# One maximum and one exponential for each head of a cached decode, with keys and values loaded apart

## The chip, the core and the metric

The kernel runs on one core of one Trainium2 chip. TensorE (PE) multiplies matrices, VectorE (DVE) reduces and combines, ScalarE (ACT) takes exponentials, GpSimd (POOL) does almost nothing here; the SyncE queue (SP) and the ScalarE queue issue the DMA transfers. A product of two float32 matrices appears in the trace as two matmul records, each with a weight load (PEld) of its own. The metric is the device time in microseconds (us) from one execution; lower is better.

## The reference

One token passes four residual layers: attention, MLP, attention, MLP, with the same weights both times. Of the attention, 32 heads of 128 numbers look at 8192 cached keys and values each:

```python
x = x + _A_ref(_layernorm(x), A_k_cache, A_v_cache, A_wq, A_wo)
x = x + _B_ref(_layernorm(x), B_w1, B_w2)
# and both once more
q = (x @ wq).reshape(B, Sq, H, Dh).transpose(0, 2, 1, 3)
scores = einsum("bhqd,bhkd->bhqk", q, k_cache) * (Dh ** -0.5)
o = einsum("bhqk,bhkd->bhqd", softmax(scores), v_cache)
attention = o.reshape(B, Sq, H * Dh) @ wo
mlp = maximum(x @ w1, 0) @ w2
```

The width of x is 640, the MLP's hidden width 1728. One head's keys and values are 8 MiB in float32, all heads together 256 MiB, and both attention layers read all of them.

## The kernel before

**The ring.** All keys and values go through one large SBUF buffer (`ring`, L70), which has room for 3712 "columns"; a column is 8 numbers in each of 128 partitions (4 KiB in all). `UNITS` (L33) cuts each head's 2048 columns (COLS, a quarter of the keys, since four groups of 32 PE columns each take a quarter) into units; a unit is one DMA and holds keys and values of the same columns side by side. A usual head has two units of two "steps" of 512 columns; the first and the last heads have smaller ones, down to 128. `place` (L81) looks for the smallest gap that holds the next unit, and `pump` (L90) issues loads on the SP queue as long as there is one; `release` (L112) frees a step's place when its values have been used, and pumps again. All this runs when the program is written, so the order of releases and loads is fixed; on the chip, a load waits until the last reader of its place has finished. Layer 0 takes heads 0 to 31, layer 1 takes them from 31 down, and what layer 0 loaded last (`KEPT`, L39, exactly one ring full: all of head 31 and most of head 30) isn't loaded again. Nothing can be loaded between the last byte of layer 0 and the first release in layer 1.

**A step** (L265) runs through these helpers: `scores` (L293) multiplies the query with the keys. For a step of 512 columns these are 16 products of 128 columns into one PSUM tile: four groups of 32 partitions, and in each of them four "rows", that is four runs of 128 keys; the query sits in column r of a 32-wide weight tile otherwise zero (`spread_q`, L287), so run r lands in row r. `maxima` (L314) takes the maximum over 128 numbers and joins it with the one of the steps before; `exponentials` (L321) takes exp with the sum, and the factor by which earlier steps have to be rescaled. `turn` (L341) transposes the 128 probabilities by a product with a 0/1 matrix and copies them to SBUF (`pT`). `values` (L357) multiplies with the values: four products of 512 columns, whose result holds for each row all four runs, of which only the row's own block counts. `rescaled` (L375) multiplies the output and the sum so far with the factor, and `gathered` (L391) adds the row's own blocks, one DVE instruction for each of four.

**A head's end.** `combined` (L418) finds the common maximum of all rows by a product that spreads them and a minimum, weighs the rows by exp, sums them by two more products and divides. That is a "chore": generators in two lists, `chores` and `slow`, which advance by one step between other work (`work_off`, L521). Other chores are the queries of the next four heads (L530), the output projection of four heads (L536), what the MLP needs before the last head is ready (`before_last`, L544) and a product of MLP weights with the last head's output weights (L444, L471), so that behind the last head there is only one product left for the MLP's hidden layer (L638).

**The order of the work** is written by hand (`manual_schedule`) and each engine takes its instructions in that order. The loop at L601 is pipelined over steps: the turn of step i, then scores, maximum and exponential of step i+1, then the values of step i, then chores and the rescaling. Behind the last step come the output of the last head (`o`, in the trace `c_ol`, L634), the rest of the MLP (L637 to L704), and in layer 0 the normalisation and first queries of layer 1 (L506 to L508), whose result is `qT` (L251).

Of the kernel before, what the change touches and what calls it, by code (L numbers as in the profile page):

```python
# [30 lines left out]

COLS = SK // 4
UNITS = {h: [[512, 512], [512, 512]] for h in range(H)}  # L33
UNITS[0] = [[128], [128], [256], [512], [512, 512]]
UNITS[29] = [[512, 512], [512], [512]]
UNITS[30] = [[256], [128], [128], [512], [512, 512]]
UNITS[31] = [[512, 512], [512], [256], [128], [128]]
RING = 3712
KEPT = [(30, i) for i in range(2, 5)] + [(31, i) for i in range(5)]  # L39
STEPS = 8  # L40
# [3 lines left out]
def rows(n):  # L44
    return 4 if n % 512 == 0 else 1
# [10 lines left out]
def decode_kernel(ctx: ExitStack, tc: tile.TileContext, x, kv, wq, wo, w1, w2, out):  # L56
# [5 lines left out]
    ps_s = ctx.enter_context(tc.tile_pool(name="ps_s", bufs=3, space=bass.MemoryType.PSUM))  # L62
# [9 lines left out]
    assert KEPT == order[len(order) - len(KEPT) :]  # L72
    todo = [(0, u) for u in order] + [(1, u) for u in order[::-1][len(KEPT) :]]
    dram_at, o = {}, 0
    for h, i in order:
        dram_at[h, i] = o
        o += 8 * P * sum(UNITS[h][i])
# [12 lines left out]
    def pump():  # L90
        while todo:
            layer, u = todo[0]
            steps = UNITS[u[0]][u[1]]
            n = sum(steps)
# [9 lines left out]
            for t, m in enumerate(steps):  # L104
                live[layer, u, t] = at, m
                at_of[layer, u, t] = 8 * at
                at += m

    def key(st):
        return (0 if st.u in KEPT else st.L), st.u, st.t  # L110

    def release(st):  # L112
        if st.L or st.u not in KEPT:
            del live[key(st)]
            pump()

# [40 lines left out]
    wct = consts.tile([P, NB, P], F32, name="wct")  # L157

# [106 lines left out]
    class Step:  # L265
        def __init__(self, L, u, t, e):
            self.L, self.u, self.t, self.e = L, u, t, e
            self.h = u[0]
            self.n = UNITS[self.h][u[1]][t]
            self.rows = rows(self.n)  # L270
            self.m = self.n // self.rows
            self.counts = ind[:, 4:5] if self.rows == 4 else ind[:, :1]

    class Head:

        def __init__(self):
            self.nm = work.tile([P, STEPS], F32, name="h_nm", bufs=2)
            self.l = work.tile([P, STEPS], F32, name="h_l", bufs=2)  # L280
            self.c = work.tile([P, STEPS], F32, name="h_c", bufs=2)
            self.sum = work.tile([P, 1], F32, name="h_sum", bufs=2)
            self.o = work.tile([P, DH], F32, name="h_o", bufs=2)

    heads_of = {}
# [7 lines left out]
    def scores(st):  # L293

        h = st.h
        st.at = at_of[key(st)]
        st.ps = bank_tile()
        for r in range(st.rows):
            for g in range(4):
                if st.rows == 1:  # L300
                    q = qT[h // HG][:, h % HG : h % HG + 1].to_broadcast([P, 32])
                else:
                    q = spread_q[h % 2][:, 3 - r : 35 - r]
                k = st.at + g * st.n + r * st.m
                nc.tensor.matmul(  # L305
                    st.ps[32 * g : 32 * g + 32, : st.m],
                    q,
                    ring[:, k : k + st.m],
                    start=(r == 0),
                    stop=(r == st.rows - 1),  # L310
                    skip_group_check=True,
                )

    def maxima(st):  # L314
        e, nm = st.e, heads_of[st.h].nm
        to = work.tile([P, 1], F32, name="s_nm", bufs=2) if e else nm[:, :1]
        nc.vector.tensor_reduce(to, st.ps[:, : st.m], AX.X, ALU.max, negate=True)  # L317
        if e:
            nc.vector.tensor_tensor(nm[:, e : e + 1], nm[:, e - 1 : e], to, op=ALU.min)  # L319
# [178 lines left out]
    def attention_and_mlp(L, xr, s):  # L498
# [92 lines left out]
        def begin(i):  # L591
            st = steps[i]
            if st.e == 0:
                due(st.h)
# [190 lines left out]
```

## Time and profile before

| what | value |
|---|---|
| median of 3 runs | 1428.64 us (1428.23 to 1429.79) |
| the profiled execution | 1427.12 us, of which 1425.3 us from the first to the last instruction (the span) |
| busy share of the span | PE 66%, PEld 39%, DVE 46%, ACT 13% |
| mean granted TensorE clock | 0.808 of full speed |
| DMA | 572.69 MB, mean 402 GB/s over the span |

In a row of the timeline the first number is the start in us from the span's start, the second its length, then engine, line, operation, result and operands, and how many records were merged (x). In a group's row stand, behind the bar, busy us and mean ns of one record, then the idle time of the engine just before them and what ended it. Records of matmuls overlap, since four groups of PE columns work side by side: x8 of the 512-column shape are four products, and the time of all eight is what counts.

### The profile page before, as it was taken

To read this page: it belongs to the slowest core of one execution; us is meant where nothing else is said; L and a number is where in the kernel's file an instruction comes from. 1 tells how busy PE (TensorE), PEld (TensorE's weight loads), DVE (VectorE), ACT (ScalarE), POOL (GpSimd) and SP (SyncE) were. 2 spreads that over 40 slices of the span, in tenths; PEclk is the share of its full clock that TensorE was granted. 3 is DMA by queue.
4 is the path that set the end of the run, shared out by engine and by line. 5 is a ranking of instruction groups with operands and counts; after the bars stand their busy time and mean duration, and the time that the engine had idled before them with its cause. 6 is when DMAs were issued, how large, how long until landed. Compare 5 with 4: busy or idle time off the path is not lost.

```text
span 1425.3 us, 30398 instructions
## 1 busy us (share of the span) xinstructions
PE 936.8 (66%) x12964; PEld 559.3 (39%) x12964; DVE 654.2 (46%) x2793; ACT 186.7 (13%) x821; POOL 2.9 (0%) x10
## 2 busy tenths in 40 slices
PE   5665546667566767666688666666657667666678
PEld 3333324344343434334345333434434344344434
DVE  2443424545444444446436544545444545445453
ACT  1111101111111111111112111111111111111110
POOL 0000000000000000000000000000000000000000
PEclk8777867888877878889768887878888887888887
DMA  9999999999999999999718999999999999999990
GB/s 398 432 432 426 428 434 428 422 427 425 425 428 428 430 419 430 431 424 423 323 53 357 427 431 430 425 429 427 419 432 431 426 421 424 431 429 427 417 418 6
DMA packets 25343, 572.69 MB, mean 402 GB/s; under 512 B 2804, under 2 KB 2936, under 8 KB 4344
## 3 DMA queue, kind: packets, MB, share of 16 engines
q1 hardware_dynamic: 20600, 524.38, 86.2%
q10 hardware_dynamic: 4608, 46.37, 7.8%
q8 instruction: 102, 1.67, 0.5%
q14 instruction: 33, 0.27, 0.0%
HBM read 570.74 MB, written 0.00 MB: 400 GB/s over the span
## 4 chain that ended last, share of the span: by engine, by line
DMA 75%; PE 20%; DVE 3%; issue 1%; ACT 0%; SPq 0%; ACTq 0%; DVEq 0%
DMA ring<-in_kv 75%; PE ps L305 8%; PE outs L365 8%; DVE h_o L398 2%; PE px L256 1%; PE acc L489 1%; PE ps L347 1%; PE px L236 0%; PE acc L256 0%; ACT p L324 0%; PE pm L406 0%; DVE s_nm L317 0%; PE ps L652 0%; PE px L476 0%; SPq L100 0%
## 5 line engine op out<-in xcount | busy, mean ns | idle before, releaser
L305 PE MATMUL ps<-ring,spread_q 128*32 128x128 f32 x8000 | 350.1, 329 | 425.5 <-DMA ring<-in_kv 425.5
L305 PEld LDWEIGHTS ps<-ring,spread_q 128*32 128x32 f32 x8000 | 267.0, 131 | 439.8 <-issue 406.1
L398 DVE SCALAR_TENSOR_TENSOR h_o<-outs,ind,h_o 128x128 f32<-128x128 f32 x954 | 334.4, 351 | 95.2 <-PE outs L365 68.3
L365 PE MATMUL outs<-ring,pT 128*4 128x512 f32 (+1 forms) x2192 | 349.5, 713 | 23.4 <-DVE pT L355 22.6
L324 ACT ACTIVATE p<-ps,h_nm 128x128 f32<-128x128 f32 (+1 forms) x268 | 99.0, 370 | 1055.3 <-DVE h_nm L319 606.5
L317 DVE TENSOR_REDUCE s_nm<-ps 128x1 f32<-128x128 f32 x204 | 59.8, 293 | 313.6 <-PE ps L305 312.8
L347 PEld LDWEIGHTS ps<-row_of,p 128*128 128x128 f32 x500 | 86.5, 209 | 151.1 <-ACT p L324 78.0
L317 DVE TENSOR_REDUCE h_nm<-ps 128x1 f32<-128x128 f32 (+1 forms) x64 | 18.8, 294 | 247.7 <-PE ps L305 247.7
L347 PE MATMUL ps<-row_of,p 128*128 128x16 f32 x500 | 97.3, 271 | 12.3 <-ACT p L324 11.9
L365 PEld LDWEIGHTS outs<-ring,pT 128*4 128x4 f32 (+1 forms) x2192 | 65.6, 101 | 48.6 <-DVE pT L355 44.0
L406 PEld LDWEIGHTS pm<-ident,h_nm 128*128 128x128 f32 x128 | 25.2, 246 | 92.5 <-issue 91.2
L333 ACT ACTIVATE h_c<-h_nm 128x1 f32<-128x1 f32 x204 | 57.6, 282 | 0.0
L380 DVE TENSOR_SCALAR h_o<-h_o,h_c 128x128 f32<-128x128 f32 x204 | 57.0, 279 | 0.0
L355 DVE COPY pT<-ps 128x16 f32<-128x16 f32 (+2 forms) x268 | 44.6, 166 | 25.0 <-PE ps L347 24.8
L324 ACT ACTIVATION_READ_ACCUMULATOR p<-ps,h_nm 128x1 f32 x268 | 51.7, 193 | 0.0
L382 DVE SCALAR_TENSOR_TENSOR h_sum<-h_l,ind,h_sum 128x1 f32<-128x1 f32 x204 | 44.8, 219 | 7.3
L381 DVE TENSOR_SCALAR h_sum<-h_sum,h_c 128x1 f32<-128x1 f32 x204 | 42.3, 207 | 0.0
L476 PE MATMUL px<-w_t,wct 128*128 128x448 f32 (+1 forms) x80 | 40.9, 595 | 0.0
L406 PE MATMUL pm<-ident,h_nm 128*128 128x128 f32 x128 | 39.9, 403 | 0.8 <-DVE h_nm L319 0.8
L427 PEld LDWEIGHTS pm<-c_w,h_sum 128*128 128x128 f32 x124 | 18.4, 187 | 52.8 <-issue 25.2
L414 ACT ACTIVATE c_w<-h_nm,c_low 128x1 f32<-128x1 f32 x64 | 18.9, 295 | 148.8 <-DVE c_low L412 148.8
L319 DVE TENSOR_TENSOR h_nm<-h_nm,s_nm 128x1 f32<-128x1 f32 x204 | 32.6, 160 | 7.0
(104 smaller groups left out, 405.9 us busy)
## 6 DMA issues: line engine op xcount, KB each, us to landing
ring<-in_kv SPq DMA_DIRECT2D x118, 4096.0 KB, 18.2
wq_t<-in_wq ACTq DMA_DIRECT2D x14, 1280.0 KB, 17.5
wo_t<-in_wo ACTq DMA_DIRECT2D x14, 1280.0 KB, 17.5
ring<-in_kv SPq DMA_DIRECT2D x8, 2048.0 KB, 21.9
ring<-in_kv SPq DMA_DIRECT2D x5, 1024.0 KB, 23.9
ring<-in_kv SPq DMA_DIRECT2D x9, 512.0 KB, 25.1
w_t<-in_w ACTq DMA_DIRECT2D x1, 4480.0 KB, 36.1
w_t<-in_w ACTq DMA_DIRECT2D x1, 4320.0 KB, 24.7
```

The costliest lines, as they stand in the source:

```text
L305: nc.tensor.matmul(st.ps[32 * g : 32 * g + 32, : st.m], q, ring[:, k : k + st.m], start=(r == 0), stop=(r == st.rows - 1), skip_group_chec ...
L317: nc.vector.tensor_reduce(to, st.ps[:, : st.m], AX.X, ALU.max, negate=True)
L324: nc.scalar.activation(st.p[:, : st.m], st.ps[:, : st.m], AF.Exp, bias=hd.nm[:, e : e + 1], scale=1.0, accum_out=hd.l[:, e : e + 1],)
L333: nc.scalar.activation(hd.c[:, e : e + 1], hd.nm[:, e - 1 : e], AF.Exp, bias=hd.nm[:, e : e + 1], scale=-1.0,)
L347: nc.tensor.matmul(pt[:, w * b : w * b + w], st.p[:, b * P : (b + 1) * P], by, start=True, stop=True,)
L355: nc.vector.tensor_copy(st.pT[:, : w * nb], pt[:, : w * nb])
L365: nc.tensor.matmul(st.out[32 * g : 32 * g + R, :R].rearrange("p r d -> p (r d)"), st.pT[:, i * R : (i + 1) * R], ring[:, v : v + R * DH], ...
L380: nc.vector.tensor_scalar(hd.o, hd.o, c, 0.0, op0=ALU.mult, op1=ALU.add)
L381: nc.vector.tensor_scalar(hd.sum, hd.sum, c, 0.0, op0=ALU.mult, op1=ALU.add)
L382: nc.vector.scalar_tensor_tensor(hd.sum, hd.l[:, e : e + 1], st.counts, hd.sum, op0=ALU.mult, op1=ALU.add)
L398: nc.vector.scalar_tensor_tensor(o, st.out[:, r], by, o, op0=ALU.mult, op1=ALU.add)
L406: nc.tensor.matmul(pt[:, :P], nm.to_broadcast([P, P]), ident, start=True, stop=True)
```

## The change

A head is no longer cut into steps that each have keys and values. It has "pieces" of keys and pieces of values, in units of their own: `UNITS[h]` is a list of (kind, pieces). A key piece is (r, c, n): columns c to c+n of run r, and there are only four runs for the whole head, of 512 columns each (`RUN`). A value piece is (b, r, m): block b of 128 keys in each of m runs from r. A usual head has one unit of keys and one of values, 1024 columns (4 MiB) each; heads 0, 1, 29, 30 and 31 have smaller ones, heads 0 and 31 end in two value units of 128.

All scores of a head go to one PSUM bank of 512 columns, four products for each key piece, and a key piece is released when its scores are done. Then one maximum and one exponential over 512 columns are taken; nothing has to be rescaled. Four blocks are turned, with one copy. `rows_weighed` finds the common maximum, the rows' weights and the sum while the turn runs, and puts 0/1 masks times weight over sum into `hd.w`. `values` adds all blocks into one PSUM bank. `output` copies that bank to SBUF, half by DVE and half by ACT, and sums each row's own block with four products of one column. The loop runs head by head: scores, maximum, exponential, turn, values, output; scores of the next head come after the output of this one. Side work is advanced between pieces. In layer 1, what was kept is taken first. `first_of_last` projects two heads of the last group a head earlier, and `before_last` yields after each of its five blocks. The ring has the same size, the kept part too; the score tiles have 2 buffers for 3, and the turned probabilities get a PSUM tile of their own.

```diff
+RUN = COLS // 4
+NBL = RUN // P
+K_ALL = [(r, 0, RUN) for r in range(4)]
+V_ALL = [(b, 0, 4) for b in range(NBL)]
+WHOLE = [("k", K_ALL), ("v", V_ALL)]
+HALVES = [("k", K_ALL[:2]), ("k", K_ALL[2:]), ("v", V_ALL[:2]), ("v", V_ALL[2:])]
+LAST = [("v", V_ALL[:2]), ("v", V_ALL[2:3]), ("v", [(3, 0, 2)]), ("v", [(3, 2, 2)])]
+UNITS = {h: WHOLE for h in range(H)}
+UNITS[0] = HALVES[:2] + LAST
+UNITS[1] = HALVES
+UNITS[29] = HALVES
+UNITS[30] = [
+    ("k", K_ALL[:1]),
+    ("k", [(1, 0, RUN // 2)]),
+    ("k", [(1, RUN // 2, RUN // 2)] + K_ALL[2:]),
+] + HALVES[2:]
+UNITS[31] = HALVES[:2] + LAST
+DROPPED = {30: 2}
 RING = 3712
...
+    def scores(hd, piece, where, first, last):
+
+        r, c, n = piece
+        at = at_of[key(*where)]
+        for g in range(4):
+            nc.tensor.matmul(
+                hd.ps[32 * g : 32 * g + 32, c : c + n],
+                spread_q[hd.h % 2][:, 3 - r : 35 - r],
+                ring[:, at + g * n : at + (g + 1) * n],
+                start=first,
+                stop=last,
+                skip_group_check=True,
+            )
+        release(*where)
+
+    def exponentials(hd):
+        nc.vector.tensor_reduce(hd.nm, hd.ps, AX.X, ALU.max, negate=True)
+        hd.p = work.tile([P, RUN], F32, name="p")
+        nc.scalar.activation(
+            hd.p, hd.ps, AF.Exp, bias=hd.nm, scale=1.0, accum_out=hd.l
+        )
+
+    def turn(hd):
+
+        pt = ps_m.tile([P, 512], F32, name="pt")
+        for b in range(NBL):
+            nc.tensor.matmul(
+                pt[:, 16 * b : 16 * b + 16],
+                hd.p[:, b * P : (b + 1) * P],
+                row_of.rearrange("p g r -> p (g r)"),
...
+        hd.pT = work.tile([P, 16 * NBL], F32, name="pT")
+        nc.vector.tensor_copy(hd.pT, pt[:, : 16 * NBL])
+
+    def rows_weighed(hd):
+
         pt = ps_m.tile([P, 512], F32, name="pm")
+        nc.tensor.matmul(pt[:, :P], hd.nm.to_broadcast([P, P]), ident, start=True, stop=True)
         low = work.tile([P, 1], F32, name="c_low")
         nc.vector.tensor_reduce(low, pt[:, :P], AX.X, ALU.min)
         w = work.tile([P, 1], F32, name="c_w")
+        nc.scalar.activation(w, hd.nm, AF.Exp, bias=low, scale=-1.0)
+        yield
+        wi = work.tile([P, 1], F32, name="c_wi")
+        nc.vector.tensor_mul(wi, w, ind[:, 4:5])
+        yield
         pt = ps_m.tile([P, 512], F32, name="pm")
+        nc.tensor.matmul(pt[:, :1], hd.l.to_broadcast([P, P]), wi, start=True, stop=True)
+        yield
         rl = work.tile([P, 1], F32, name="c_r")
         nc.vector.reciprocal(rl, pt[:, :1])
+        nc.vector.tensor_scalar(hd.w, ind[:, :4], w, rl, op0=ALU.mult, op1=ALU.mult)
+
+    def values(hd, piece, where, first, last):
+        b, r, m = piece
+        at = at_of[key(*where)]
+        for g in range(4):
+            i = 4 * b + g
+            v = at + g * m * DH
+            nc.tensor.matmul(
+                hd.out[32 * g : 32 * g + 4, r : r + m].rearrange("p r d -> p (r d)"),
+                hd.pT[:, 4 * i : 4 * i + 4],
+                ring[:, v : v + m * DH],
...
+        release(*where)
+
+    def output(hd, col):
+
+        oc = work.tile([P, 4, DH], F32, name="p")
+        nc.vector.tensor_copy(oc[:, :2], hd.out[:, :2])
+        nc.scalar.copy(oc[:, 2:], hd.out[:, 2:])
+        yield
+        pt = ps_m.tile([P, 512], F32, name="pm")
+        for r in range(4):
+            nc.tensor.matmul(
+                pt[:, :1], oc[:, r], hd.w[:, r : r + 1], start=(r == 0), stop=(r == 3)
+            )
+        nc.vector.tensor_copy(col, pt[:, :1])
...
+        for where, h in enumerate(heads):
+            due(h)
+            hd = Head(h)
+            pieces = list(pieces_of(L, h, "k"))
+            for a, (piece, at) in enumerate(pieces):
+                scores(hd, piece, at, a == 0, a == len(pieces) - 1)
+                if a < len(pieces) - 1:
+                    side_work()
+            exponentials(hd)
+            side_work()
+            if h == last:
+                side_work()
+            weighing = rows_weighed(hd)
+            next(weighing)
+            turn(hd)
+            next(weighing)
+            next(weighing)
+            hd.out = outs[count[0] % 2]
+            count[0] += 1
+            pieces = list(pieces_of(L, h, "v"))
+            for a, (piece, at) in enumerate(pieces):
+                values(hd, piece, at, a == 0, a == len(pieces) - 1)
+                if a == 0:
+                    at_once(weighing)
+                    if h != last:
+                        spread(heads[where + 1])
+                if a < len(pieces) - 1 and (h != last or a == 1):
+                    side_work()
+            if h == last:
+                o = work.tile([P, 1], F32, name="c_ol")
+                rest = output(hd, o)
+                next(rest)
+                side_work()
+                at_once(rest)
+            else:
+                k, j = divmod(where, HG)
+                at_once(output(hd, o_cols[k][:, j : j + 1]))
```

More of the change, by code (lines that the diff above doesn't have):

```diff
@@ L92, in pump @@
             layer, u = todo[0]
[L93 to L94 removed]
+            kind, pieces = unit = UNITS[u[0]][u[1]]
+            n = size(unit)
             at = place(n)
@@ L103, in pump @@
             )
-            for t, m in enumerate(steps):
+            for t, piece in enumerate(pieces):
+                m = wide(kind, piece)
                 live[layer, u, t] = at, m
@@ L107, in pump, with key, release, pieces_of @@
                 at += m
[L109 to L114, printed above, removed]
-            pump()
+    def key(L, u, t):
+        return (0 if u in kept else L), u, t
+    def release(L, u, t):
+        if L or u not in kept:
+            del live[key(L, u, t)]
+            pump()
+    def pieces_of(L, h, kind):
+        units = [i for i in range(len(UNITS[h])) if UNITS[h][i][0] == kind]
+        if L:
+            units.sort(key=lambda i: (h, i) not in kept)
+        for i in units:
+            for t, piece in enumerate(UNITS[h][i][1]):
+                yield piece, (L, (h, i), t)
     wq_t, wo_t = {}, {}
@@ L291, in spread @@
         )
[L293 to L312, printed above, removed]
@@ L341, in turn @@
-    def turn(st):
-        pt = st.ps[:, 256:]
-        nb, w = st.m // P, 4 * st.rows
-        by = row_of.rearrange("p g r -> p (g r)") if st.rows == 4 else sel[:, :4]
-        for b in range(nb):
+    def scores(hd, piece, where, first, last):
[11 more added lines that the diff above has]
+        release(*where)
@@ L614, in attention_and_mlp, with side_work @@
-        while chores:
+        def side_work():
             work_off("pe")
             work_off("dve")
-        assert not slow
-        st, hd = steps[-1], heads_of[last]
-        nm = hd.nm[:, st.e : st.e + 1]
-        pt = spread_maxima(nm)
-        turn(st)
-        w = weights(nm, pt)
-        values(st)
-        rescaled(st)
-        po = ps_m.tile([P, 512], F32, name="pm")
-        nc.tensor.matmul(po[:, :1], hd.sum.to_broadcast([P, P]), w, start=True, stop=True)
-        gathered(st)
@@ L630, in attention_and_mlp @@
-        rl = work.tile([P, 1], F32, name="c_r")
-        nc.vector.reciprocal(rl, po[:, :1])
-        nc.tensor.matmul(po[:, 1:2], hd.o, w, start=True, stop=True)
-        o = work.tile([P, 1], F32, name="c_ol")
-        nc.vector.tensor_mul(o, po[:, 1:2], rl)
-        del heads_of[last]
+        spread(heads[0])
+        for where, h in enumerate(heads):
[33 more added lines that the diff above has]
+            else:
+                k, j = divmod(where, HG)
+                at_once(output(hd, o_cols[k][:, j : j + 1]))
@@ L637, in attention_and_mlp @@
+        assert not chores and not slow
         xp, ph = mlp_in
```

223 lines of the change are left out of this document (50 added, 173 removed).

## The prediction

> **What bounds the kernel now.** I read the page first: the forty slices, the DMA queues and the chain that ended last.
>
> ```profile
> span 1425.3 us, 30398 instructions
> PE 936.8 (66%) x12964; PEld 559.3 (39%) x12964; DVE 654.2 (46%) x2793; ACT 186.7 (13%) x821; POOL 2.9 (0%) x10
> GB/s 398 432 432 426 428 434 428 422 427 425 425 428 428 430 419 430 431 424 423 323 53 357 427 431 430 425 429 427 419 432 431 426 421 424 431 429 427 417 418 6
> q1 hardware_dynamic: 20600, 524.38, 86.2%
> q8 instruction: 102, 1.67, 0.5%
> DMA 75%; PE 20%; DVE 3%; issue 1%; ACT 0%; SPq 0%; ACTq 0%; DVEq 0%
> ring<-in_kv SPq DMA_DIRECT2D x118, 4096.0 KB, 18.2
> wq_t<-in_wq ACTq DMA_DIRECT2D x14, 1280.0 KB, 17.5
> wo_t<-in_wo ACTq DMA_DIRECT2D x14, 1280.0 KB, 17.5
> ```
>
> Two plateaus near 427 GB/s, one hole in the middle, one at the end. Then the stretches (columns: busy time of PE, PEld, DVE, ACT, POOL with instruction counts, granted clock, DMA share, GB/s).
>
> ```profile
> 50.00:700.00 650.00, 412.50 (x5762) 245.54 (x5762) 294.21 (x1241) 83.23 (x368) 0.00 (x0) 0.80 1.00 427
> 706.00:708.00 2.00, 2.00 (x46) 1.30 (x42) 0.95 (x6) 0.00 (x0) 0.00 (x0) 1.00 0.06 20
> 708.00:740.00 32.00, 27.06 (x336) 16.01 (x332) 12.46 (x61) 3.33 (x15) 1.10 (x2) 0.78 0.01 1
> 740.00:758.00 18.00, 13.76 (x190) 8.28 (x182) 8.47 (x40) 3.47 (x16) 0.00 (x0) 0.63 0.55 185
> 758.00:775.00 17.00, 12.24 (x192) 6.39 (x188) 13.75 (x60) 4.35 (x21) 0.00 (x0) 0.96 1.02 434
> 1390.00:1392.00 2.00, 2.00 (x46) 1.45 (x50) 0.60 (x4) 0.00 (x0) 0.00 (x0) 1.00 0.11 45
> 1392.00:1425.30 33.30, 26.65 (x286) 14.22 (x278) 12.12 (x58) 3.33 (x15) 0.55 (x1) 0.74 0.01 2
> ```
>
> From 50 to 700 us the DMA share is 1.00: the engines there wait for bytes, and what they save is worth nothing. The last bytes of layer 0 land at about 706.5, those of layer 1 at about 1390.5 (after 706 and 1390 only 40 and 90 KB come). Until 740, and to the end, nothing is moved. So the time is bytes at 427 GB/s plus two holes, and an edit counts only if it shortens a hole, removes bytes, or makes PE slower than the DMA. Then the timeline at the holes.
>
> ```profile
> 722.65 0.16 DVE L634 TENSOR_TENSOR c_ol<-pm,c_r 128x1 f32<-128x1 f32 x1 [0.47 <-PE pm L632]
> 741.51 0.16 DVE L251 COPY qT<-px 128x4 f32<-128x4 f32 x1 [0.68 <-PE px L248]
> 745.00 44.59 SPq L100 DMA_DIRECT2D ring<-in_kv  x8
> 1381.79 1.93 PE L305 MATMUL ps<-ring,spread_q 128*32 128x128 f32 x32 [2.13 <-DMA ring<-in_kv]
> 1390.73 1.08 PE L305 MATMUL ps<-ring,spread_q 128*32 128x128 f32 x32
> 1408.67 0.16 DVE L634 TENSOR_TENSOR c_ol<-pm,c_r 128x1 f32<-128x1 f32 x1 [0.47 <-PE pm L632]
> ```
>
> The last wait for data ends at 1381.79. When the last bytes land, PE is still scoring an earlier step (1390.73): of the last head a row-split step, then steps of 256, 128 and 128 columns are to follow, each with its own scores, maximum, exponential, turn, values and rescaling. The last head's output (c_ol) is ready at 722.81 and 1408.83: 16.3 and 18.3 us after the last byte.
>
> **Prices for the change.**
>
> ```profile
> L305 PE MATMUL ps<-ring,spread_q 128*32 128x128 f32 x8000 | 350.1, 329 | 425.5 <-DMA ring<-in_kv 425.5
> L317 DVE TENSOR_REDUCE s_nm<-ps 128x1 f32<-128x128 f32 x199 | 57.7, 290 | 310.6 <-PE ps L305 309.8
> L317 DVE TENSOR_REDUCE s_nm<-ps 128x1 f32<-128x256 f32 x5 | 2.1, 425 | 3.0 <-PE ps L305 3.0
> L324 ACT ACTIVATE p<-ps,h_nm 128x128 f32<-128x128 f32 (+1 forms) x268 | 99.0, 370 | 1055.3 <-DVE h_nm L319 606.5
> L324 ACT ACTIVATE p<-ps,h_nm 128x256 f32<-128x256 f32 x6 | 2.8, 473 | 19.8 <-DVE h_nm L319 18.0 <-DVE h_nm L317 1.7
> L647 DVE COPY wct<-acc 128x256 f32<-128x256 f32 x2 | 0.8, 424 | 3.7 <-PE acc L489 3.7
> L236 PE MATMUL px<-wq_t,ln_xc 128*32 128x128 f32 x640 | 26.8, 327 | 1.8 <-DMA wq_t<-in_wq 1.8
> L476 PE MATMUL px<-w_t,wct 128*128 128x448 f32 (+1 forms) x80 | 40.9, 595 | 0.0
> L256 PE MATMUL acc<-wo_t,o_cols 128*32 128x160 f32 x496 | 23.0, 325 | 1.4 <-DVE o_cols L432 1.4
> 501.90 2.00 PE L365 MATMUL outs<-ring,pT 128*4 128x512 f32 x8
> 505.67 1.04 PE L365 MATMUL outs<-ring,pT 128*4 128x512 f32 x8 [0.33 <-DVE pT L355]
> 713.70 2.42 PE L489 MATMUL acc<-w_t,ln_xc 128*32 128x448 f32 x24
> 716.05 0.61 PE L347 MATMUL ps<-sel,p 128*128 128x4 f32 x4
> 748.72 1.01 PE L347 MATMUL ps<-sel,p 128*128 128x4 f32 x4 [0.99 <-ACT p L324]
> ```
>
> A "piece" of the new kernel is four products of 512 columns, for scores as for values; the trace has that shape in L365 (x8, two records to a product): 1.04 us at the full clock, 2.00 at half. A maximum over 512 columns: 0.29 for 128 and 0.425 for 256, so 0.135 for each further 128, estimate 0.70. The exponential likewise: 0.37 and 0.47, estimate 0.68. The turn of four blocks is twice the x4 rows: 1.2 us, or 2.0 at half. The copy of half an output is 0.42 (L647), and the four products that sum rows are priced like the turn, 1.2 to 2.0 (same 128x128 weights, few columns).
>
> **Steady state: worth nothing.** Fewer score products, rescalings and row gathers free PE, and DVE most of all; all of it lies under the DMA. But the pipelining is gone: before, the next step's scores stood between turn and values (L603); now PE goes scores, maximum and exponential (waited for), turn, copy, values, copy of the output, sums, in one line for each head. At the full clock: 4 x 1.04 + about 4 (0.70 + 0.68 + 0.3 hand-overs + 1.2 + 0.4 for pT + 0.7 for the weighing product that stands ahead of values) + 4 x 1.04 + 1.9 = 14.2 us. Side work (L236, L256, L476: 91 us over 64 heads) adds 1.4: 15.6. The DMA needs 8192 KB plus a quarter of 2560 KB a head, 9.04 MB at 427 GB/s: 21.2 us. With two cold pieces of four in scores and in values, and the chain at half, it is 15.6 + 4 x 0.96 + 1.5 = 21 at worst, some of the side work inside the wait for maximum and exponential, so I take 19. The ring still holds three units of 1024 columns: K's place is released at the end of scores, V's at the end of values, and since a load takes the smallest gap that holds it, each release issues the load after the next two, so that PE may lag a landing by nearly two loads (about 20 us) before the queue runs dry. I take 0 us; bounds: no gain (share 1.00), a loss as in rival A.
>
> Here the clock decides, so two stretches after a wait of 3.7 us, and the one after c_ol:
>
> ```profile
> 500.40:504.00 3.60, 3.57 (x41) 1.89 (x41) 1.04 (x6) 0.64 (x3) 0.00 (x0) 0.54 1.03 439
> 504.20:507.00 2.80, 2.47 (x44) 1.26 (x43) 2.42 (x12) 0.64 (x3) 0.00 (x0) 1.00 1.10 433
> 722.60:736.00 13.40, 13.12 (x147) 8.12 (x146) 2.48 (x14) 0.37 (x2) 0.55 (x1) 0.50 0.01 2
> ```
>
> A burst begins at 0.54 and is at 1.00 after 3.6 us; a PE that falls behind waits less and so stays fast. The last row warns: 13 us of busy PE at 0.50. The Trainium skill ("TensorE: Matmul & The Clock Gate", "HAM oscillation — how this bites in real kernels") says that waits longer than some 3.4 us bring the clock to half, so that every burst starts cold. The trace agrees with that in the first two rows and not with the page's opening after one busy window in the third; by the rule alone both bursts of each head would start cold, which is the 21 us above.
>
> **Bytes.** The ring, the kept share (3712) and all loads are as large as before. Of 30398 instructions about half go: scores from 8000 matmul records (L305) to 2048 (64 heads, 16 products of two records) with as many weight loads, DVE from 2793 / 64 = 44 a head, side work included, to some 12. The instruction queue's 0.5% of the span (7 us) would lose up to half: between 0 (if these packets fill idle slots) and 3.5 us; I take 1.5.
>
> **The end of a layer.** Let T be the last byte. The last head's second K half lands 9.8 us earlier (4.19 MB at 427). Two pieces and one of the MLP's blocks (2.42 / 3 = 0.8 us): 2.9 to 5.6 us. Maximum, exponential, with two more blocks and the maxima's spreading under them: 2.1. Turn 1.2 to 2.0, pT 0.4, weighing 0.7. Values can start between T-2.6 and T+1. Five pieces, of which the last two are halves, and a block: 2 x 1.04 + 0.8 + 1.04 + 1.04 = 5, the end between T+2.4 and T+6. Output: the last block 0.8 covers the copies, the sums 1.2, the column's copy 0.3: 2.3. c_ol' is ready between T+4.7 and T+8.3; I take T+6, nearer the fast end, as these bursts are dense. No score, maximum or exponential is left behind T. That wins 18.3 - 6 = 12.3 at the end and 16.3 - 6 = 10.3 between the layers; sum 22.6, bounds 18 to 25. From c_ol to the queries (qT ends at 741.67) nothing changes: 18.9 us.
>
> **The restart.** Before, the hole's edge 740 to 758 ran at 185 GB/s: 18 x (427 - 185) / 427 = 10.2 us lost, since the first load waits for scores, exponential, turn and values of a 128-column step (745.00) and its place takes only 128 columns. Now a K piece is released right behind its scores: one copy of the spread query (0.2) and a cold piece (2.0) give the first load, of 1 MB, at 744.0. Then, by the same placing: 0.5 MB behind piece 2, 2 MB behind piece 4 (748.5), 2 MB behind the second value piece (4 us chain and 2.7: 755.3), twice 2 MB in head 30's scores (from 760), and the first 4 MB only behind head 30's last value piece (about 772.5). Between them the DMA rests 0.8, 1.9 and 2.5 us; with 1.9 around the weights' load at 740.40 that is 7.1. Gain 3; bounds -3 (both heads at half clock) and 6.
>
> **Sum.** The profiled execution took 1427.12 us (span 1425.3 and 1.8 around it), 1.5 below the median of the runs. 1427.1 - 12.3 - 10.3 - 3 - 1.5 = 1400.0; on the median 1401.5. I forecast 1402.
>
> **Rivals.**
> A. PE becomes the bound, slower than before. Scores and values no longer overlap the wait for maximum and exponential. For: the row at 722.6, and 21 us against 21.2. Against: bursts of the 512-column shape reach 1.00 in 3.6 us. It decides from 21.2 us a head; one us more costs 54 us over the 54 whole heads (2 to 28 in both layers): 1402 + 54 = 1456; at the half clock throughout (about 25 us) some 1600. Break-even lies 0.5 us a head above 21.2.
> B. The tail is won only in part: PE enters the last head late (it lags by a head's output and the projections, about 6 us) and c_ol' comes at T+12. Then 10.6 instead of 22.6: 1414. For: PE works near the DMA's pace. Against: the last two heads are loaded in halves, which lets it start earlier, and the weights' loads are over by then.
> C. The clock stays open behind c_ol', because denser work precedes it. The 13.4 us at 0.50 take then some 4 us less in each layer: 1394. Against: the row shows that density of records did not open it.
>
> **How the numbers follow.** Forecast 0.67, its own range 1395 to 1411; A 0.12; B 0.13; C 0.08. Range 1394 to 1419: it holds C's edge, the forecast and most of B, and leaves A out. Less than 0.2% (2.9 us), about what a measurement of this kernel can tell from no change, needs A to cancel the gain: 0.03. Of A the rest, 0.09, is slower; faster 0.88.
>
> **What would show it.** Right: in the windows of after, share 1.00 on both plateaus and PE waiting for DMA once or twice a head; c_ol some 6 us after the last byte in both layers; the first ring load about 2.3 us after qT; fewer MB on the instruction queue. Wrong: ring waits of PE gone from the plateaus and GB/s below 427 there (A); PE's last wait for data in a layer long before the last byte (B); a granted clock above 0.6 behind c_ol (C).

## The result and the profile after

The kernel after takes 1380.57 us (median of 4 runs, 1378.0 to 1382.41) against 1428.43 of the kernel before in the same comparison: a ratio of 0.9664 (95% interval 0.9645 to 0.9682), 48 us faster. The forecast was 1402 with a range of 1394 to 1419: right in direction, and the gain nearly twice as large. The profiled execution took 1378.0 us with a span of 1376.2.

From the page of after, some of the lines that the prediction shows of before:

```profile
span 1376.2 us, 15734 instructions
PE 985.7 (72%) x7120; PEld 384.0 (28%) x7120; DVE 174.9 (13%) x679; ACT 100.3 (7%) x273; POOL 2.9 (0%) x10
...
GB/s 393 432 432 426 433 430 433 428 427 435 429 429 430 430 430 431 431 430 425 427 168 411 426 433 431 430 426 432 432 430 430 432 426 434 429 430 431 431 423 171
...
q8 instruction: 55, 0.90, 0.3%
q14 instruction: 11, 0.09, 0.0%
```

Half of the instructions are gone, and the holes of the GB/s line have shrunk: 168 and 171 where 53 and 6 stood. Then the stretches of after (columns as before: PE, PEld, DVE, ACT, POOL with counts, granted clock, DMA share, GB/s), and four of before that the prediction did not show:

```profile
40.00:690.00 650.00, 456.23 (x3118) 172.85 (x3122) 76.90 (x287) 46.25 (x126) 0.00 (x0) 0.78 1.00 430
690.00:704.00 14.00, 11.31 (x112) 4.62 (x104) 2.44 (x10) 1.07 (x3) 0.00 (x0) 1.00 0.67 280
704.00:720.00 16.00, 12.82 (x230) 9.00 (x234) 4.70 (x25) 0.74 (x3) 1.10 (x2) 1.00 0.04 7
718.57:753.57 35.00, 29.01 (x260) 12.08 (x260) 6.66 (x24) 2.89 (x8) 0.00 (x0) 0.90 0.98 392
753.57:1345.00 591.43, 428.80 (x2948) 163.62 (x2948) 73.31 (x275) 44.80 (x122) 0.00 (x0) 0.79 1.00 430
1350.00:1355.00 5.00, 4.06 (x24) 1.28 (x28) 0.00 (x0) 0.00 (x0) 0.00 (x0) 0.66 0.82 338
1360.00:1374.00 14.00, 12.38 (x202) 7.50 (x194) 3.29 (x17) 0.74 (x3) 0.55 (x1) 1.00 0.00 1
```
```profile
690.00:706.50 16.50, 12.51 (x174) 6.39 (x170) 9.93 (x42) 2.68 (x12) 0.00 (x0) 0.84 0.85 358
740.40:775.40 35.00, 26.05 (x372) 15.07 (x372) 22.22 (x99) 7.82 (x35) 0.00 (x0) 0.79 0.78 310
775.40:1375.00 599.60, 396.20 (x5582) 237.77 (x5582) 281.48 (x1187) 79.27 (x350) 0.00 (x0) 0.82 1.00 427
1375.00:1390.00 15.00, 11.50 (x154) 6.68 (x150) 8.70 (x36) 2.35 (x12) 0.00 (x0) 0.79 0.94 396
```

Three things stand in them. Behind the last byte the granted clock is 1.00 (704 to 720, 1360 to 1374), where it was 0.50. The 35 us from the first weight load of layer 1 move 392 GB/s where they moved 310. And the plateaus run at 430 instead of 427, of which the last 14 us of layer 0 return a part (280 GB/s: the last loads trickle in). The timeline at the holes:

```profile
704.11 0.61 PE L372 MATMUL outs<-ring,pT 128*4 128x256 f32 x8 [0.63 <-DMA ring<-in_kv]
704.79 0.42 DVE L385 COPY p<-outs 128x256 f32<-128x256 f32 x1 [4.70 <-PE outs L372]
705.39 1.05 PE L390 MATMUL pm<-h_w,p 128*128 128x1 f32 x8
706.48 0.16 DVE L393 COPY c_ol<-pm 128x1 f32<-128x1 f32 x1 [1.27 <-PE pm L390]
712.87 1.84 PE L286 MATMUL px<-w_t,hT 128*32 128x160 f32 x48
719.48 0.16 DVE L281 COPY qT<-px 128x4 f32<-128x4 f32 x1 [0.48 <-PE px L278]
721.88 46.57 SPq L119 DMA_DIRECT2D ring<-in_kv  x10
1364.89 0.16 DVE L393 COPY c_ol<-pm 128x1 f32<-128x1 f32 x1 [1.26 <-PE pm L390]
```

In layer 0 PE takes the very last half piece at 704.11, right as it lands. The 24 products of w2 (L286, 48 records) take 1.84 us; before, this block took nearly twice as long:

```profile
732.83 3.42 PE L256 MATMUL px<-w_t,hT 128*32 128x160 f32 x48
```

From these rows and the trace's landing records the span falls into six parts (c_ol and qT are taken at their ends, 0.16 us behind the starts). The last bytes land at 707.5 and 1391.5 in before and at 704.1 and 1360.7 in after; the prediction read 706.5 and 1390.5 off stretches of 2 us, a microsecond early in both layers.

| part | before | after | difference | forecast |
|---|---|---|---|---|
| start to last byte of layer 0 | 707.5 | 704.1 | -3.4 | about -0.75 |
| last byte to c_ol | 15.4 | 2.6 | -12.8 | -10.3 |
| c_ol to the queries of layer 1 (qT) | 18.9 | 13.0 | -5.9 | 0 |
| qT to last byte of layer 1 | 649.8 | 641.1 | -8.7 | -3.75 |
| last byte to c_ol | 17.3 | 4.3 | -13.0 | -12.3 |
| c_ol to the end | 16.5 | 11.2 | -5.3 | 0 |

The forecast column shares its 1.5 us for bytes out over the two layers. Of the -8.7, the first 35 us bring 35 x (392 - 310) / 427 = 6.7.

### The profile page after: what moved, and what is told of

Its sections match the earlier page's. It is cut to its first block, busy times and chain, and to the rows that moved or that the text cites. A ratio compares the mean times of both kernels' runs of the same rounds, so it can differ in the third digit from the quotient of the medians.

```text
span 1376.2 us, 15734 instructions
## 1 busy us (share of the span) xinstructions
PE 985.7 (72%) x7120; PEld 384.0 (28%) x7120; DVE 174.9 (13%) x679; ACT 100.3 (7%) x273; POOL 2.9 (0%) x10
## 2 busy tenths in 40 slices
DMA packets 26570, 571.74 MB, mean 415 GB/s; under 512 B 2948, under 2 KB 3080, under 8 KB 4360
## 4 chain that ended last, share of the span: by engine, by line
DMA 71%; PE 26%; DVE 1%; ACT 1%; issue 0%; SPq 0%; ACTq 0%; DVEq 0%
DMA ring<-in_kv 71%; PE ps L316 9%; PE outs L372 9%; PE px L439 2%; PE px L266 1%; PE pt L337 1%; PE acc L286 1%; ACT p L329 1%; DVE h_nm L327 1%; PE px L286 1%; PE acc L452 1%; PE pm L360 0%; DVE pT L345 0%; PE pm L390 0%; PE px L278 0%
## 5 line engine op out<-in xcount | busy, mean ns | idle before, releaser
L316 PE MATMUL ps<-ring,spread_q 128*32 128x512 f32 x2064 | 333.9, 774 | 202.7 <-DMA ring<-in_kv 202.2
L316 PEld LDWEIGHTS ps<-ring,spread_q 128*32 128x32 f32 x2064 | 68.2, 134 | 348.7 <-DMA ring<-in_kv 210.6
L372 PEld LDWEIGHTS outs<-ring,pT 128*4 128x4 f32 x2080 | 57.9, 103 | 261.0 <-issue 201.0
L327 DVE TENSOR_REDUCE h_nm<-ps 128x1 f32<-128x512 f32 x64 | 44.3, 692 | 479.2 <-PE ps L316 479.2
L329 ACT ACTIVATE p<-ps,h_nm 128x512 f32<-128x512 f32 x64 | 44.0, 687 | 704.8 <-DVE h_nm L327 694.1
L390 PE MATMUL pm<-h_w,p 128*128 128x1 f32 x512 | 69.2, 256 | 34.5 <-DVE p L385 34.2
L390 PEld LDWEIGHTS pm<-h_w,p 128*128 128x128 f32 x512 | 63.6, 192 | 95.9 <-DVE p L385 95.5
L337 PE MATMUL pt<-row_of,p 128*128 128x16 f32 x512 | 69.3, 267 | 23.6 <-ACT p L329 23.6
L337 PEld LDWEIGHTS pt<-row_of,p 128*128 128x128 f32 x512 | 63.1, 194 | 35.4 <-ACT p L329 35.4
L266 PE MATMUL px<-wq_t,ln_xc 128*32 128x128 f32 x640 | 34.9, 396 | 1.9 <-DMA wq_t<-in_wq 1.9
L266 PEld LDWEIGHTS px<-wq_t,ln_xc 128*32 128x32 f32 x640 | 29.6, 165 | 19.8 <-issue 16.5
L286 PE MATMUL acc<-wo_t,o_cols 128*32 128x160 f32 x496 | 33.3, 435 | 0.0
L286 PEld LDWEIGHTS acc<-wo_t,o_cols 128*32 128x32 f32 x496 | 23.2, 161 | 22.2 <-issue 17.0
```

What stands on the lines that cost most here:

```text
L266: nc.tensor.matmul(pq[32 * j : 32 * j + 32, :DH], xc[:, c : c + 1].to_broadcast([P, 32]), wq_t[g][:, c, j * DH : (j + 1) * DH], start=(c = ...
L286: nc.tensor.matmul(acc[32 * g : 32 * g + 32, :DR], col.to_broadcast([col.shape[0], 32]), wt[:, g * DR : (g + 1) * DR], start=first, stop=last,
L316: nc.tensor.matmul(hd.ps[32 * g : 32 * g + 32, c : c + n], spread_q[hd.h % 2][:, 3 - r : 35 - r], ring[:, at + g * n : at + (g + 1) * n], ...
L327: nc.vector.tensor_reduce(hd.nm, hd.ps, AX.X, ALU.max, negate=True)
L329: nc.scalar.activation(hd.p, hd.ps, AF.Exp, bias=hd.nm, scale=1.0, accum_out=hd.l)
L337: nc.tensor.matmul(pt[:, 16 * b : 16 * b + 16], hd.p[:, b * P : (b + 1) * P], row_of.rearrange("p g r -> p (g r)"), start=True, stop=True,)
```

## Experiments: the clock behind the last head

Theory: rival C. The same MLP and normalisation follow c_ol in both kernels, and the difference is whether the work ahead of it leaves the clock open. So one run breaks the dense work in the new kernel, and one adds dense work to the old kernel.

**A pause ahead of c_ol.** 36 small VectorE instructions keep the last head's sums waiting:

```diff
+GAP = 36
...
+                for _ in range(GAP):
+                    nc.vector.tensor_scalar(
+                        hd.w, hd.w, 1.0, 0.0, op0=ALU.mult, op1=ALU.add
+                    )
                 at_once(rest)
```

> The changed kernel with 36 tiny DVE multiplications by one between the copies of the last head's output and its sums, in both layers, so that PE idles there. They cost some 5 us a layer by themselves (about 0.14 us each). Theory: the clock stays open behind c_ol only because dense work stands just ahead of it; the idle closes it, and the stretches c_ol to qT and c_ol to the end go back from 13.0 and 11.2 us to about 18.9 and 16.5: 1380.6 + 10 + 11 = 1402. Rival: what opens the clock there is something else (the phase of its windows): 1391, granted clock 1.00 behind c_ol.

Measured: 1404.1 us, ratio 0.9831 (0.9817 to 0.9846). Its timeline, and a stretch of it:

```profile
711.85 1.87 PE L391 MATMUL pm<-h_w,p 128*128 128x1 f32 x8 [7.04 <-DVE h_w L587]
713.76 0.16 DVE L394 COPY c_ol<-pm 128x1 f32<-128x1 f32 x1 [1.96 <-PE pm L391]
730.32 0.16 DVE L282 COPY qT<-px 128x4 f32<-128x4 f32 x1 [0.68 <-PE px L279]
1386.23 0.16 DVE L394 COPY c_ol<-pm 128x1 f32<-128x1 f32 x1 [1.96 <-PE pm L391]
```
```profile
709.00:724.00 15.00, 11.87 (x122) 8.00 (x126) 4.83 (x28) 0.37 (x2) 0.14 (x1) 0.54 0.01 1
```

PE rests 7.04 us and then runs at 0.54, and the same four products (eight records) take 1.87 us, not 1.05. From c_ol to qT it is 16.6 us (13.0), from c_ol to the end of the span (1402.5) 16.1 (11.2). So of the 23.5 us lost, 3.6 + 4.9 come behind c_ol, from the clock alone; nearly all of the rest is the two pauses and the slower products right behind them. The Trainium skill ("TensorE: Matmul & The Clock Gate", "What's actually happening") says that an idle window of some 3.4 us brings the clock to half; the row agrees.

**Dense products in the kernel before**, ahead of its c_ol, into a bank nobody reads:

```diff
+        def dense():
+            pt = ps_m.tile([P, 512], F32, name="px")
+            for g in range(4):
+                nc.tensor.matmul(
+                    pt[32 * g : 32 * g + 32, :],
+                    ident[:, :32],
+                    w1_t[:, 0, :512],
+                    start=True,
+                    stop=True,
+                )
...
+                if i >= len(steps) - 4:
+                    dense()
...
         values(st)
+        dense()
```

> The kernel before with five groups of four dense products (512 columns, 1 us at the full clock, results unused) put between the last four steps of a layer's last head and behind its last values. Theory: they keep the clock open, c_ol to qT falls from 18.9 to about 13 and c_ol to the end from 16.5 to about 11; the fillers cost 1 to 2 us each layer since PE waits 0.6 us at each place anyway: 1428.4 - 11 + 3 = 1420. Rival: the clock closes all the same, and the fillers are only paid for: 1431.

Measured: 1422.51 us, ratio 0.9961 (0.9946 to 0.9976). Stretches and timeline:

```profile
722.60:736.00 13.40, 10.92 (x208) 7.83 (x204) 3.91 (x24) 0.37 (x2) 1.10 (x2) 1.00 0.00 1
1406.50:1420.00 13.50, 11.95 (x146) 7.42 (x146) 2.71 (x15) 0.37 (x2) 0.55 (x1) 0.62 0.00 1
```
```profile
723.88 0.16 DVE L648 TENSOR_TENSOR c_ol<-pm,c_r 128x1 f32<-128x1 f32 x1 [0.47 <-PE pm L646]
736.90 0.16 DVE L251 COPY qT<-px 128x4 f32<-128x4 f32 x1 [0.69 <-PE px L248]
```

The old kernel now runs from c_ol to qT in 13.0 us, as fast as the new one, at a clock of 1.00. In layer 1 the clock closes midway (0.62) and little is won. So the 5.9 us in layer 0 are the clock: the filler wins all of them, and the pause gives 3.6 of them back. In layer 1 the pause gives back 4.9 of 5.3, and the filler wins only about 1. Note that the stretch 722.6 to 736 of before, at 0.50, had more busy time of PE (13.12 us) than this one (10.92): at half the clock each record takes longer, so a busy share read there did not tell which way the clock goes.

## Experiments: what is loaded last, and how soon the ring is free

**Keys last.** Half of K, all of V, then the other half of K, in the first and last heads:

```diff
+KLAST = [HALVES[0], HALVES[2], HALVES[3]]
+KLAST += [("k", K_ALL[2:3]), ("k", [(3, 0, RUN // 2)]), ("k", [(3, RUN // 2, RUN // 2)])]
-UNITS[0] = HALVES[:2] + LAST
+UNITS[0] = KLAST
-UNITS[31] = HALVES[:2] + LAST
+UNITS[31] = KLAST
```

> The changed kernel with the last head's loads of both layers in another order: half the keys, all values, then the other keys in pieces of 1, 0.5 and 0.5 MB, so that scores, maximum, exponential, turn and values of the head stand behind the last byte. Theory (the tail is won by keys that land before the values): last byte to c_ol takes 12 to 14 us for 2.7 and 5.1, 1380.6 + 18 = 1399. Rival (it is won by fewer and denser instructions, in whatever order the bytes come): within 5 us of 1380.6.

Measured: 1403.54 us, ratio 0.9825 (0.9805 to 0.9845). Its stretch and timeline:

```profile
703.40:716.40 13.00, 11.92 (x108) 6.05 (x100) 2.26 (x8) 1.44 (x4) 0.00 (x0) 0.90 0.00 0
```
```profile
716.30 0.16 DVE L395 COPY c_ol<-pm 128x1 f32<-128x1 f32 x1 [1.16 <-PE pm L392]
729.29 0.16 DVE L283 COPY qT<-px 128x4 f32<-128x4 f32 x1 [0.48 <-PE px L280]
```

Nothing is moved after 703.4, and c_ol is ready 13.1 us later (2.6 in after), while c_ol to qT stays at 13.0. That is 10.5 us lost in layer 0; with 9.0 in layer 1 (1371.9 to 1385.2, that is 13.3 for 4.3) it is nearly all of the 20.2 us between the two profiled executions (1398.17 and 1378.0; 23 us between the medians). Maximum, exponential, turn and values stand behind the last byte again. So keys before values, and not the single maximum by itself, is what shortens the end of a layer.

**Late release.** In layer 1, head 31's key places are freed only behind its first value piece:

```diff
-        release(*where)
+        if where[0] == 1 and hd.h == H - 1:
+            held.append(where)
+        else:
+            release(*where)
```

> The changed kernel, in which layer 1 gives back the places of its first head's keys only behind that head's first value piece (as a head that frees keys and values together would). Theory: the first load of layer 1 is issued some 9 to 10 us behind qT for 2.2, the DMA rests about 7 us longer: 1387. Rival: the refill is bound later, by the first 4 MB load that waits for head 30's values; then under 1383.

Measured: 1386.53 us, ratio 0.9709 (0.9691 to 0.9726). Timeline, and the 35 us from the same point as in after, 1.07 us ahead of the end of qT (719.33):

```profile
730.14 28.91 SPq L119 DMA_DIRECT2D ring<-in_kv  x8
```
```profile
718.26:753.26 35.00, 29.97 (x260) 12.29 (x260) 5.84 (x23) 2.89 (x8) 0.00 (x0) 0.86 0.73 301
```

The first load goes out 10.8 us behind qT, not 2.2, and these 35 us move 301 GB/s, as in before (310). That costs 6 us, close to the 6.7 that the restart won.

## Experiments: what the plateaus gained

Three GB/s more on some 1240 us are 0.7%, more than the forecast's term for bytes. One theory was the shape of the loads, the other the instructions, whose queues (8 and 14) stand on the page beside those of the data.

**Smaller loads in the kernel before**, so that more of them wait in the queue:

```diff
-UNITS = {h: [[512, 512], [512, 512]] for h in range(H)}
+UNITS = {h: [[512], [512], [512], [512]] for h in range(H)}
...
-UNITS[29] = [[512, 512], [512], [512]]
```

> The kernel before with units of one step (2 MB) for the heads 1 to 29, so that each load is issued as soon as one step's place is free; instructions as before. Rival of the instruction theory: the deeper queue brings the plateaus from 427 to 430 GB/s, -8 us, 1420. Instruction theory: plateaus at 427, within 2 us of 1428 but for the restart of layer 1, which may win up to 3.

Measured: 1433.86 us, ratio 1.0048 (1.0031 to 1.0065), 426 GB/s on both plateaus. It is 5 us slower, where 1420 or about 1428 was expected. More and earlier loads do not raise the rate; but the packets became more and smaller (41761, for 25343 in before and 26570 in after), so this run doesn't clear the shape of the loads altogether.

**More instructions in the kernel after**, ahead of a layer's last four heads: on GpSimd 170 fills of one number a head, on VectorE 115 or 47 such fills, 23 copies of 128x256, or 47 copies of 128x128.

```diff
+EXTRA = 24, 23
...
+    def dve_work(n):
+        for _ in range(n):
+            nc.vector.memset(idle, 0.0)
...
                     at_once(weighing)
...
+                    if where < H - 4:
+                        dve_work(EXTRA[0])
...
+                if where < H - 4:
+                    dve_work(EXTRA[1])
```

This is the one with 47 fills; the copies stand at the same two places.

> The changed kernel with 170 one-number memsets on GpSimd for each head but the last four of a layer (9520 in all, on an engine that is idle), which bring back 0.6 of the 0.95 MB of instructions that the change saved. Theory: the rise from 427 to 430 GB/s on the plateaus comes from fewer instruction fetches; then 428 GB/s and 1380.6 + 5 = 1386. Rival: it comes from loads that are issued earlier, so that the queue is deeper; then 430 GB/s and 1381 to 1382.

> The changed kernel with 115 one-number memsets on DVE for each head but the last four of a layer (6440 in all, 60 behind the first value piece and 55 behind a head's output, where DVE waits), 59 ns each by the page of before. In a_small 9520 such instructions on GpSimd raised queue q14 from 0.09 to 0.70 MB and each layer's transfers took some 20 us longer. Theory: the fetches of q14 lie on few of the sixteen DMA engines, the slowest of which sets the end; q14 then shows 0.5 MB, the plateaus fall below 430 GB/s, and the time rises by 20 to 30 us (1400 to 1410). Rival: in a_small it was GpSimd's writes or its late power instruction; then 1381 to 1384 here.

> The changed kernel with 23 DVE copies of 128x256 in SBUF for each head but the last four of a layer, at the places of a_tiny: about as much DVE time, a fifth of the instructions, far more bytes in SBUF. Theory (instruction fetches): +2 to +4 us, plateaus at 429 to 430. Rival: DVE's traffic in SBUF slows the transfers that land there; then plateaus near 427 or below and more than 1385.

> The kernel after with 47 fills of one number on VectorE in each of the 56 heads ahead of a layer's last four, 2632 in all: about as many as VectorE and ScalarE lost by the change (3614 to 952). They take some 3 us of VectorE a head, under the load of 21. Theory: the plateaus' 427 to 430 GB/s come from the instructions that are no longer fetched on these engines. Then queue 14 goes from 0.09 to about 0.25 MB, the plateaus fall to 425 to 428 GB/s, and the time is 1388 to 1400 us. Rival, that the plateaus gained by TensorE's missing instructions, or by the shape of the loads: queue 14 grows the same, the plateaus stay at 430 and the time at 1379 to 1383.

> The kernel after with 47 copies of 128x128 numbers on VectorE in each of the 56 heads, 24 and 23 at the two places where the fills of one number stood: as many instructions as those 2632, but each about three times as long (some 0.17 us for 0.06), so that they come at a third of the pace, nearer to how VectorE and ScalarE issued the instructions that the change took away. Theory that an instruction costs the transfers a fixed time however densely it stands: queue 14 near 0.26 MB, the last byte of layer 0 at 708 to 710 us, the time 1388 to 1396 us as with the fills. Rival, that only the dense bursts hurt, so that the fewer instructions of the change explain little of its gain on the plateaus: queue 14 the same, last byte 703 to 705 us, time 1379 to 1384 us.

| added | DVE busy | queue 14 | c_ol, layer 0 | time | ratio (interval) |
|---|---|---|---|---|---|
| nothing | 175 us | 0.09 MB | 706.6 | 1380.57 | 0.9664 (0.9645 to 0.9682) |
| 1288 copies of 128x256 | 541 us | 0.17 MB | 707.7 | 1381.27 | 0.9669 (0.9650 to 0.9688) |
| 2632 fills | 323 us | 0.26 MB | 712.1 | 1393.45 | 0.9762 (0.9739 to 0.9785) |
| 2632 copies of 128x128 | 756 us | 0.26 MB | 712.2 | 1396.27 | 0.9785 (0.9767 to 0.9803) |
| 6440 fills | 544 us | 0.51 MB | 729.3 | 1430.20 | 1.0021 (1.0007 to 1.0035) |
| 9520 fills on GpSimd | 175 us | 0.70 MB | 726.7 | 1443.87 | 1.0112 (1.0097 to 1.0127) |

The groups of the 1288 copies, of the 2632 copies and of the 6440 fills, and the instruction queue with the 2632 fills:

```profile
L402 DVE COPY idle<-idle 128x256 f32<-128x256 f32 x1288 | 377.4, 293 | 40.2
```
```profile
L402 DVE COPY idle<-idle 128x128 f32<-128x128 f32 x2632 | 596.7, 227 | 86.8
```
```profile
L401 DVE MEMSET idle<- 1x1 f32 x6440 | 380.0, 59 | 341.8
```
```profile
q14 instruction: 32, 0.26, 0.1%
```

The time that VectorE works is no cause: 377 us of copies cost 0.7 us, 380 us of fills cost 50. Nor is the pace: 2632 fills of 59 ns and 2632 copies of 227 ns put c_ol of layer 0 at the same 712.1 and 712.2, and cost 13 and 16 us. Their number counts, and not in proportion (1288 cost next to nothing). In size the theory failed at both ends: 9520 and 6440 fills cost far more than was expected, 1288 copies less. The one with 6440 fills moves its data more slowly; the two with 2632 still show 429 GB/s on the plateau and lose it at its end, here of the copies:

```profile
40.00:690.00 650.00, 440.61 (x2982) 168.59 (x2982) 252.87 (x3391) 44.44 (x121) 0.00 (x0) 0.78 1.00 420
```
```profile
700.00:704.00 4.00, 4.00 (x41) 1.38 (x34) 0.69 (x1) 0.69 (x2) 0.00 (x0) 1.00 0.25 101
704.00:708.00 4.00, 3.62 (x35) 2.01 (x39) 1.04 (x5) 0.39 (x2) 0.00 (x0) 1.00 0.06 27
708.00:710.00 2.00, 2.00 (x32) 0.84 (x28) 0.00 (x0) 0.00 (x0) 0.00 (x0) 1.00 0.03 12
```

The kernel after has taken its last half piece at 704.11; this one still moves 27 and then 12 GB/s, with nearly all its data in: the last load's sixteen parts no longer land together. In the trace's landing records they come 10.4 us apart (699.1 to 709.5); in after 7.0 (697.0 to 704.1). Fifteen of them are in by 703.3 and one comes 6.2 us later; with 6440 fills it is one part, too, 10.2 us behind the other fifteen. And 27 GB/s is a sixteenth of 430, which fits one of the sixteen DMA engines still at work alone; why it falls behind is not shown.

The packet records go with the number of instructions too. Between 20 and 690 us, 18 packets of 32 KiB take more than 1.3 us in after (1.2 is usual), 23 with the 1288 copies, 65 and 60 with the 2632 fills and copies, 363 with the 6440 fills; in before it is 117, and 30 with the added products of TensorE below.

The GpSimd run is worth less than the others: behind its last fills a GpSimd instruction that layer 1 needs came 26.5 us late, so its time has a second cause.

**TensorE's share.** 26 products of one column a head, behind the first value piece; they go into a bank that other sums use, so its output is not the reference's.

```diff
+SMALL = 26
...
+                    if where < H - 4:
+                        for _ in range(SMALL):
+                            nc.tensor.matmul(
+                                acc[:32, 500:501], ident[:, :32], ones, start=True, stop=True
+                            )
```

> The kernel after with 26 products of one column on TensorE in each of the 56 heads ahead of a layer's last four, behind the first value piece: some 2900 more records of TensorE (products and weight loads), about half of what the change took away there. They cost 1 to 2 us of TensorE a head, while it waits 3 to 4 us for data in every head. Theory that TensorE's instruction queue (8) counts too: it goes from 0.90 to about 1.3 MB, the plateaus fall below 430 GB/s and the time is 1384 to 1390 us. Rival, that only the fetches of VectorE and ScalarE hurt: 1379 to 1383 us and 430 GB/s. If TensorE itself became late, its waits for the ring would shrink below 100 us in all.

Measured: 1389.2 us, ratio 0.9736 (0.9717 to 0.9755). Its queue and stretches:

```profile
q8 instruction: 78, 1.28, 0.4%
```
```profile
40.00:690.00 650.00, 522.68 (x4494) 243.04 (x4494) 76.58 (x285) 45.88 (x125) 0.00 (x0) 0.74 1.00 429
719.70:754.70 35.00, 30.48 (x270) 15.46 (x274) 4.76 (x19) 2.52 (x7) 0.00 (x0) 0.70 0.85 323
754.70:1340.00 585.30, 494.86 (x4295) 231.35 (x4287) 72.36 (x269) 43.74 (x119) 0.00 (x0) 0.75 1.00 427
```

The products took 2.7 us of PE a head, more than meant, and the restart suffers from that (323 for 392 GB/s, 35 x 69 / 430 = 5.6 us of the 8.6 lost). What is left is about 3 us, and the plateau of layer 0 lost next to nothing (c_ol at 707.6 for 706.6). Whether TensorE's fetches count stays open.

## Experiment: the half clock in the last head

In after, the stretch 1350 to 1355 runs at 0.66, behind a wait of 1.90 us for the second half of K. Dense products into an unused bank, behind the key pieces 0 and 1, were to keep the clock open:

```diff
+FILL = 1
...
+                if h == last and a in (0, 1):
+                    for _ in range(FILL):
+                        dense()
```

> The kernel after with four dense products of 512 columns (into a bank nobody reads) ahead of the score pieces 0 and 1 of a layer's last head, so that the granted clock stays at 1.00 through the wait for the second half of K. Theory: the pieces that run at half the clock near 1350 us make the last head of layer 1 about 2 us late; with the filler c_ol there comes 1 to 3 us after the last byte (5 before) and the time is 1376 to 1379 us. Rival, that the last value pieces and not the clock set c_ol's time: no change, or up to 1 us later by the filler itself: 1380 to 1382 us.

Measured: 1383.59 us (1377.11 to 1386.27), ratio 0.9690 (0.9666 to 0.9715). It overlaps the interval of after: no gain can be told. In the profiled execution the stretch 1350 to 1355 did run at 1.00, c_ol of layer 1 came 0.5 us sooner behind the last landing than in after (3.8 for 4.3), and c_ol to qT took 14.6 us instead of 13.0.

## Why the prediction was right or wrong

**What bounds the kernel: right.** Bytes plus two holes; 43.7 of the 49.1 us between the profiled executions lie in the holes and in the restart beside them.

**Steady state worth nothing, rival A: right that PE is not the bound.** PE's waits in after (us in total, times, longest):

```profile
PE ps L316 <- DMA ring<-in_kv: 202.2, 64, 6.9
PE outs L372 <- DMA ring<-in_kv: 47.8, 30, 8.9
```

It waits once in each of the 64 heads for keys and in about half of them for values. The prices of the wide instructions were right too, by these groups:

```profile
L327 DVE TENSOR_REDUCE h_nm<-ps 128x1 f32<-128x512 f32 x64 | 44.3, 692 | 479.2 <-PE ps L316 479.2
L329 ACT ACTIVATE p<-ps,h_nm 128x512 f32<-128x512 f32 x64 | 44.0, 687 | 704.8 <-DVE h_nm L327 694.1
```

0.69 for an estimate of 0.70 and 0.69 for 0.68, extrapolated from widths of 128 and 256.

**From c_ol to the queries, and on to the end, nothing changes: wrong.** This is the step that failed, and the largest: 11.2 of the 22.0 us by which the profiled execution (1378.0) came out below the sum (1400.0). The others are 3.9 for bytes and instructions, 3.7 for the restart and 3.2 for the ends of the layers. Rival C had the step, at a chance of 0.08 and 4 us a layer. The prediction had the stretch at 0.50 in hand, read it as a property of that work, and took it against C. But the row held only work behind c_ol, and the same work ran at 1.00 in after and behind the filler. What decides lies ahead of it: the filler of dense products there opens the stretch, and the pause closes it. In before, though, no such pause stood there. This is PE's longest rest between the last byte and c_ol of layer 0:

```profile
710.43 1.70 PE L489 MATMUL acc<-w_t,ln_xc 128*32 128x448 f32 x16 [1.36 <-DVE ln_xc L198]
```

So a long rest is not what closed the clock in before; that its products were short and thin fits the filler's run, but which property of them counts is not shown. Nor is the stretch at 1.00 every time in the kernel after: in three runs whose edits leave the last values and all behind them alone (the last-head filler, the 1288 copies, the 2632 fills) the clock closes for 3.4 us, 3 to 4 us behind c_ol of layer 0, and c_ol to qT takes 14.6 us. So the step is worth 4.3 to 5.9 us there, and of the 3.6 that the pause gives back up to 1.6 can come without it. As the range reached to 1394 for C alone, and not for C together with the full end of a layer, it missed.

**The end of a layer: mechanism right, size off.** 2.6 and 4.3 us where T+6 was taken and T+4.7 the fast end. The estimate let values start between T-2.6 and T+1 and put five pieces, two of them halves, and an MLP block behind that. In layer 0 values start at 699.5, that is T-4.6, and every piece but the last is done when the last byte lands (704.1), so only a half piece, the copies, the sums and the column's copy are left. In layer 1 c_ol comes 1.7 us later; pieces at 0.66 of the clock stand ahead of it, but the filler meant to mend that won only 0.5 us, so the reason isn't settled (the runs with 1288 and with 2632 copies, which leave this alone, take 2.6 and 2.7 there). The term is worth 25.8 us for 22.6, just past its upper bound of 25, and that although T was read a microsecond early in both layers. Rival B falls with the same rows.

**The restart: right mechanism, low in size.** The first load goes out 2.2 us behind qT, as worked out (2.3). The gain is 6.7 us for 3, just past the upper bound of 6; the late release gives 6 by another way. The clock of that stretch is 0.90 and not near half, which the stages of the working (a cold piece, 2.0) did not grant.

**Bytes and instructions: mis-sized.** 1.5 us were taken, at most 3.5, by the share of the instruction queue's packets. Beside the restart, start to last byte and the rest of layer 1 give 3.4 + 2.0 = 5.4. The queue's share is not the price of an instruction: 2632 instructions on VectorE bring 0.17 MB more, which is 0.4 us at 427 GB/s (6.4 at a sixteenth of it, if all of them fell to one DMA engine, an estimate that no run here tests), and they cost 13 to 16 us. VectorE and ScalarE together lost 2662 (3614 to 952), about as many, so in size their number is enough to explain what the plateaus won. The form differs: with the 2632 the plateau stays at 429 GB/s and one part of the last load comes late, while before ran at 427 throughout and landed the sixteen parts of its last load within 4.4 us. So the cause of the gain on the plateaus stays open; the loads' shape changed too.

## What to carry to other kernels

Where two holes in a stream of bytes set the time, load last what has the shortest way to the result (here values, not keys), and free a buffer's places as early as their last use allows. A stage's clock can depend on what runs ahead of it: a row at half the clock says what that kernel did, not what the work needs, so a change that puts dense work, or no pause, ahead of a serial stage may be worth much behind it. And under a stream that is bound by DMA, fewer instructions can be worth more than their fetched bytes: here added ones cost more.

## What was not expected of the hardware

Added instructions cost far more than their bytes: 4.9, 6.0 and 7.7 ns of the whole kernel's time for each one added on VectorE (12.9 us / 2632 fills, 15.7 us / 2632 copies, 49.6 us / 6440 fills), whether fill or copy, while 1288 of them cost 0.7 us in all. The Trainium skill ("Runtime: NRT & Kernel Launch", "Instruction fetch mechanics") calls the cost of crossing into an engine's next block of instructions "mostly hidden"; in this case, where all DMA engines are busy, added instructions cost 13 to 50 us, though no run here shows that it is by that refill. The runs show the cost, the slow packets, the one landing that falls behind, and the instruction queue that grows with them, but not the link between them: every execution here was recorded by the profiler, so an instruction's record may have a share that these runs can't tell from its fetch.
